# Pacing a transformer's FFN pieces by their TensorE time, and projecting the second head group while rows are still being normalised

## The chip, the cores and the metric

One core of one Trainium2 chip. The metric is the time of the whole program on the device, in microseconds (us), median of several runs.

## The reference

Two identical layers on one sequence of 2048 rows of 512 columns: attention with 32 heads of 16 columns, then a gated FFN of width 1792. The same weights serve both layers.

```python
def _A_ref(x, wqkv, wo):                       # attention, H = 32, Dh = 16
    q, k, v = split_heads(x @ wqkv)            # (shortened)
    p = softmax(q @ k.T * Dh ** -0.5)
    return (p @ v).merge_heads() @ wo

def _B_ref(x, w_gate, w_up, w_down):           # FFN, F = 1792
    return (gelu(x @ w_gate) * (x @ w_up)) @ w_down

x = x + _A_ref(layernorm(x)); x = x + _B_ref(layernorm(x))
x = x + _A_ref(layernorm(x)); x = x + _B_ref(layernorm(x))
```

## The kernel before

The program is written by a scheduler in Python. It keeps a rough clock of every engine while it emits instructions, and at each step it decides what TensorE does next. What it emits is a fixed order per engine, with semaphores between the engines.

A unit is four heads times one block of 512 query rows. It has 64 score tiles of 128 keys by 512 queries. There are 8 units in a block, 4 blocks in a layer, 4096 tiles in all. A score tile is one matmul, then an exponential, then an accumulating matmul with V. Most exponentials run on ScalarE, three and two tiles at a time. Some tiles go to VectorE, which makes the exponential by integer arithmetic; such a tile needs four accumulating matmuls instead of one.

Everything else has to fit between the score tiles, in "pieces" of TensorE work with their evacuations on VectorE. There are three sources of pieces, asked in this order: `heads` (the first layer norm), `prep` (the projections Q, K and V), and `post` (all that follows the attention of a block: output projection, layer norm, gate, up, down, and the next layer norm). A piece is emitted only if its bank and inputs are ready and if it does not overrun the next score tile by more than its source's tolerance.

```python
SW, MM = 0.107, 0.216                      # the scheduler's costs, us
DVE_LATE = 2.0                             # VectorE gets a score tile if less late than this

def prep_list(layer):                      # order and gates of Q, K, V pieces  (cut)
    def kv(c, b, after_all=False):
        def gate():
            return ("xnt", layer, b) in have and (not after_all or started_all()) and (
                not layer or units_done[layer - 1] >= (NQB - 1) * NG + 2 * c + 2)
        ...
    def q(up):
        def gate():
            return ("xnt", layer, up // NCK) in have and (layer or not up or started_all()) and filled_units[0] >= ...
        ...
    for up in range(1, NU // 2):
        if up < NCK and up not in cl:
            for b in range(NQB):
                kv(up, b, layer == 0)      # head groups 1..3 of layer 0: after all rows are normalised
        ...

def post_source():
    while True:
        if posts:
            pace["on"], pace["n"] = True, 0
            ...
            for p in posts.pop(0):
                if p is not None:
                    pace["n"] += 1         # one per piece, whatever its length
                yield p
            ...

PIECES = 4 + 8 + 4 * NFT                   # 68 pieces of a post; NFT = 14

def behind():                              # pieces due by now, minus pieces done
    if not pace["on"]:
        return 0.0
    f = (tiles_filled[0] / (4.0 * NKT) - NG * (posts_done[0] + 1) - 1.0) / (NG - 1.5)
    return PIECES * f - pace["n"]

def post_tol():
    if pace["haste"] or behind() > LAG:    # LAG = 24
        return 99.0
    return 1.0 if behind() > 0 else 0.1

sources = [Source(heads(), lambda: 0.1), Source(prep_source(), lambda: 0.1), Source(post_source(), post_tol)]

while True:                                # main loop  (cut)
    ...                                    # a score tile if one is ready, or accumulating matmuls
    cand = None
    for src in sources:
        p = src.peek()
        if p is None:
            continue
        bs = piece_banks(p)
        if bs is None or piece_ready(p, bs) > t + 0.02 or p.cost + change("full") > limit + src.tol():
            continue
        cand = (src, p, bs)
        break
    ...                                    # else more accumulating matmuls, or a zero-adding filler
```

Of the kernel before, what the change touches and what calls it, by code (L numbers as in the profile page):

```python
# [175 lines left out]
def _emit_fast(nc, es, x_in, wqkv, wo, wg, wu, wd, out, n_rep=2):  # L176
# [12 lines left out]
    NCK = D // 128  # L189
    NG = 2 * NCK  # L190
    NFT = F // 128
# [4 lines left out]
    NU = NQB * NG  # L196
# [40 lines left out]
    NQS = 6  # L237
# [43 lines left out]
    SW, MM = 0.107, 0.216  # L281
# [192 lines left out]
    pace = {"on": False, "n": 0, "haste": False}  # L474
    have = set()
# [152 lines left out]
    def qproj(layer, up):  # L628

        qb, c = up // NCK, up % NCK  # L630

        def evac(b):
            ops = []
            for p in range(2):
                slot = (layer * NU + 2 * up + p) % NQS
                ops.append((lambda e, p=p, slot=slot: e.tensor_scalar(Q[:, slot, :], bank(b), QMASK[:, p:p + 1], None,  # L636
                                                                     op0=ALU.mult),
                            [BK[b], ("QMASK",)], [("Q", slot)], 0.62))
            evac_job(1, b, ops, got((layer, "q", up)))
        return mm_piece([(WQ[:, ck, 128 * c:128 * (c + 1)], XNT[:, ck, 512 * qb:512 * (qb + 1)]) for ck in range(NCK)],  # L640
                        xk(qb) + [("WQ", c)], evac)

    def kproj(layer, c, kb):
        return mm_piece([(WK[:, ck, 128 * c:128 * (c + 1)], XNT[:, ck, 512 * kb:512 * (kb + 1)]) for ck in range(NCK)],
                        xk(kb) + [("WK", c)],
                        lambda b: evac_job(1, b, [(lambda e: e.tensor_copy(KT[:, c, 512 * kb:512 * (kb + 1)], bank(b)),
                                                   [BK[b]], [("KT", c, kb)], 0.6)], got((layer, "k", c, kb))))
# [3 lines left out]
    def vproj(layer, c, kb):  # L651
        def fn(e, bs):
            for t in range(4):
                for ck in range(NCK):
                    tt = 4 * kb + t
                    ins = e.matmul(bank(bs[0])[:, 128 * t:128 * (t + 1)], lhsT=XNT[:, ck, tt * 128:(tt + 1) * 128],  # L656
                                   rhs=WV[:, ck, 128 * c:128 * (c + 1)], start=(ck == 0), stop=(ck == NCK - 1))
            return ins

        def then(o):  # L660
            have.add((layer, "v", c, kb))
            for part, (m0, m1) in (("A", (0, NMA)), ("B", (NMA, NM))):
                if m1 == m0 or kb != (3 * m1 - 1) // 4:
                    continue
                for ph in range(1, NPH):
                    dst = VD[:, c, ph - 1, :, 4 * m0:4 * m1, :]
                    src = AP(VP, (2 * c * NKT * 4 + 12 * m0 + 2) * VW,
                             [[VP[:].ap[0][0], 128], [NKT * 4 * VW, 2], [3 * VW, 4 * (m1 - m0)], [1, VW]])
                    job("pool", 2, [(lambda e, dst=dst, src=src, ph=ph: e.tensor_scalar(  # L669
                        dst, src, 2.0 ** (-ph / NPH), None, op0=ALU.mult),  # L670
                        [("VP", c, k) for k in range(kb + 1)] + [("VPONE",)], [("VD", c, part)],
                        0.46 + 0.039 * 4 * (m1 - m0))],
                        got((layer, "vd", c, part)) if ph == NPH - 1 else None)

        def after(bs):
            b = bs[0]
            evac_job(1, b, [(lambda e: e.tensor_copy(  # L677
                VP[:, c, :, 16 * kb:16 * kb + 16, 0:16].rearrange("p r k d -> p k r d"),
                bank(b).rearrange("p (k r d) -> p k r d", r=2, d=16)),
                             [BK[b]], [("VP", c, kb)], 0.6)], then)  # L680

        return Piece(0.064 * 4 * NCK, xk(kb) + [("WV", c)], fn, after)


    units_done = [0] * n_rep
    filled_units = [0]

    def started_all():
        return ("xnt", 0, NQB - 1) in have

    def prep_list(layer):
        items = []

        def add(gate, fn):
            items.append((gate, fn))
# [5 lines that stand above are left out]
            add(gate, lambda: kproj(layer, c, b))  # L701
            if b == 0 and c in cl:
                q(c)
            add(gate, lambda: vproj(layer, c, b))

        def q(up):
            def gate():
                return ("xnt", layer, up // NCK) in have and (layer or not up or started_all()) and filled_units[0] >= layer * NU + 2 * up + 2 - NQS
            add(gate, lambda: qproj(layer, up))

        lead = [b for b in range(NQB) if not layer or b < NQB - 1 or NQB == 1]
        cl = range(min(NCK, NPART // 2)) if layer else [0]
        for c in cl:
            for b in lead:
                kv(c, b)
        for b in range(NQB):
            if b not in lead:
                for c in cl:
                    kv(c, b)
        for up in range(1, NU // 2):  # L720
            if up < NCK and up not in cl:
                for b in range(NQB):
                    kv(up, b, layer == 0)
            if up not in cl:
                q(up)
        return items
# [307 lines left out]
    slot_no = [0]  # L1034
    tiles_filled = [0]
    LAG = 24
    pt_no = [0]
    dg = {"n": 0, "items": [], "uk": None, "done": [0]}
    pp_no = [0]
# [12 lines left out]
    def slot_cap():  # L1052
        bs = slot_banks()
        return len([b for b in bs if b not in held3])

    def vector_tile():

        if pace["haste"]:
            return False
        if not dg["items"] and pend.get(("PI", dg["n"] % NPI)):  # L1060
            return False
        late = max(0.0, sch.free["dve"] - now[0]) + sum(op[3] for j in jobs["dve"] for op in j[2])
        late += 0.6 * len(shifts)
        return late < DVE_LATE

    def vector_bank():
        if not free_banks:
            return None
        return min(free_banks, key=lambda b: (sch.ready("pe", w=[BK[b]]), b))
# [8 lines left out]
    def pick(look=False):  # L1078

        cap = slot_cap()  # L1080
        want_d = not look and started_all() and behind() < LAG and vector_tile()
        bd = vector_bank() if want_d else None
# [308 lines left out]
    for layer in range(n_rep):  # L1391
        prep.extend(prep_list(layer))
# [14 lines left out]
# [4 lines that stand above are left out]
                pace["haste"] = posts_done[0] % NQB == NQB - 1 and NQB > 1  # L1411
                for p in posts.pop(0):
                    if p is not None:
                        pace["n"] += 1
                    yield p
                posts_done[0] += 1
                pace["haste"] = pace["on"] = False
            else:
                yield None

    posts_done = [0]

    PIECES = 4 + 8 + 4 * NFT

    def behind():

# [6 lines that stand above are left out]
        if pace["haste"] or behind() > LAG:  # L1433
# [4 lines that stand above are left out]
    total_posts = n_rep * NQB  # L1438
    DENSE = 0.7
    log = {"idle": 0.0, "warm": 0}  # L1440

    while True:
# [40 lines left out]
        for src in sources:  # L1483
            p = src.peek()
# [7 lines left out]
        if cand:  # L1492
            src, p, bs = cand
# [775 lines left out]
def _build(nc, x_in, wqkv, wo, wg, wu, wd, out, n_rep=2, force_general=False):  # L2269

    with contextlib.ExitStack() as es:
        fast, flag = _emit_fast(nc, es, x_in, wqkv, wo, wg, wu, wd, out, n_rep=n_rep)
# [94 lines left out]
```

## Time and profile before

| | before |
|---|---|
| median, range | 1685.4 us, 1682.9 to 1685.6 |
| span of the profiled run | 1682.9 us |
| ScalarE: first exponential starts, last ends | 17.67 us, 1610.1 us |
| ScalarE busy with exponentials | 1487.9 us, 1302 instructions, 3253 tiles |
| ScalarE waits for score matmuls | 42.5 us in 71 gaps, longest 5.34; one of them, 3.90 us, stands before the first exponential |
| tail after the last exponential | 72.8 us |

From the page of the kernel before, the span, the busy time of each engine, and three groups of instructions. A group's columns are: line, engine, operation, output and input, shapes, count, then busy us, mean ns of one, then the idle time just before them and what ended it.

```profile
span 1682.9 us, 37093 instructions
...
PE 1576.2 (94%) x15611; PEld 492.6 (29%) x15670; DVE 1378.6 (82%) x2334; ACT 1561.6 (93%) x1348; POOL 203.4 (12%) x217
...
L1204 ACT ACTIVATE fPT<-fPS 128x1536 bf16<-128x1536 f32 (+1 forms) x1302 | 1487.9, 1284 | 46.3 <-PE fPS L1191 42.5
L1241 DVE TENSOR_SCALAR fPI<-fPS 128x512 int16<-128x512 f32 x843 | 571.0, 684 | 93.4 <-PE fPS L1191 87.6
...
L1344 PE MATMUL fPS<-fONB,fZV 128*17 128x512 f16 x2452 | 189.6, 385 | 2.3 <-POOL fQMASK L362 1.5
...
```

The reader should see two things. TensorE and ScalarE are both busy for nine tenths of the span, but not with work of the same kind: 2452 of TensorE's matmuls (189.6 us of its busy time) are fillers that add zero, so TensorE has room. ScalarE between its first and last exponential has almost none: its groups show 1487.9 us of exponentials and 46.3 us of idle time before them. The ScalarE timeline shows these gaps and what each waited for. Its columns are start, length, instruction, count of merged instructions, and in brackets the idle time before the first of them and its releaser.

```profile
...
47.52 23.20 ACT L1204 ACTIVATE fPT<-fPS 128x1024 bf16<-128x1024 f32 x21 [1.28 <-PE fPS L1191]
76.06 68.55 ACT L1204 ACTIVATE fPT<-fPS 128x1536 bf16<-128x1536 f32 x60 [5.34 <-PE fPS L1191]
145.66 3.71 ACT L1204 ACTIVATE fPT<-fPS 128x1536 bf16<-128x1536 f32 x3 [1.05 <-PE fPS L1191]
...
298.04 9.14 ACT L1204 ACTIVATE fPT<-fPS 128x1536 bf16<-128x1536 f32 x8 [0.40 <-PE fPS L1191]
307.66 5.97 ACT L1204 ACTIVATE fPT<-fPS 128x1536 bf16<-128x1536 f32 x5 [0.47 <-PE fPS L1191]
313.65 1.28 ACT L1157 ACT_TABLE_LOAD   x1
314.94 6.27 ACT L1157 ACTIVATE fHT<-fHT 128x3584 bf16<-128x3584 bf16 x2
...
821.87 5.54 ACT L1204 ACTIVATE fPT<-fPS 128x1024 bf16<-128x1024 f32 x5 [4.79 <-PE fPS L1191]
...
```

The larger gaps are 1.28, 5.34, 1.05 and 0.91 us in the first 151 us, 4.79 us at 817 to 822 us, where the second layer begins, and two of 1.07 and 1.18 us later. The lines from 298 to 315 us show the other kind: gaps of 0.4 us one after another in the stretch before a GELU. (The last lines of that stretch also price the change of activation table: a load of 1.28 us between the exponential and the GELU.)

What TensorE does at the 5.34 us gap, from its timeline:

```profile
...
72.48 1.04 PE L592 MATMUL fPS<-fXNT,fWQ 128*128 128x512 f16 x4
73.35 1.03 PE L592 MATMUL fPS<-fXNT,fWK 128*128 128x512 f16 x4
74.21 1.06 PE L656 MATMUL fPS<-fWV,fXNT 128*128 128x128 bf16 x16
75.61 0.40 PE L1191 MATMUL fPS<-fQ,fKT 32*128 32x512 f16 x4 [0.34 <-DVE fKT L646]
...
```

Q, K and V of the second head group are projected one after the other, VectorE evacuates Q (two products from 73.55 us, 1.41 us together) and K (fKT, 0.68 us from 74.88), and only then does a score tile follow, at 75.61 us. The first two units hold 128 tiles and are used up here.

### The profile page before, as it was taken

The page shows a single profiled execution, that of the slowest core. Times are in us where ns is not written, and L with a number is a line of the kernel's source. Part 1 is how long each engine was busy: PE and PEld are TensorE (multiplying, and loading weights), DVE is VectorE, ACT ScalarE, POOL GpSimd, SP SyncE. Part 2 cuts the span into 40 slices and gives each one's busy share as a digit, 9 for nine tenths or more (in the row PEclk, how much of TensorE's full clock was granted, in tenths as well). Part 3 has the DMA queues.
Part 4 walks back from the last instruction along what each step waited for, and adds up shares of the span by engine and source line. Part 5 has one row for each costly group of instructions (what it writes and reads, how often), then busy time and mean ns, then how long its engine had stood idle before and what let it go on. Part 6 is the DMA issues. An engine that isn't in the chain of part 4 may idle for free.

```text
span 1682.9 us, 37093 instructions
## 1 busy us (share of the span) xinstructions
PE 1576.2 (94%) x15611; PEld 492.6 (29%) x15670; DVE 1378.6 (82%) x2334; ACT 1561.6 (93%) x1348; POOL 203.4 (12%) x217
## 2 busy tenths in 40 slices
PE   9999989999999989999999999999989999999998
PEld 3332222222222223233332322222222222222233
DVE  7899998888998899977643899988899878897852
ACT  6899999999999999999899999999999999999922
POOL 2312011101201021000600211101011100201000
PEclk9999999999999999999999999999999999999999
DMA  4100001252013410125214000024301251014303
GB/s 138 52 2 19 2 19 33 61 164 73 17 43 119 144 42 10 41 66 170 74 57 138 26 19 17 21 58 136 108 19 39 68 166 57 17 45 146 109 15 109
DMA packets 140286, 111.82 MB, mean 66 GB/s; under 512 B 13905, under 2 KB 129873, under 8 KB 140113
## 3 DMA queue, kind: packets, MB, share of 16 engines
q1 hardware_dynamic: 136416, 104.78, 21.3%
q0 software_dynamic: 2112, 4.19, 0.9%
q8 instruction: 127, 2.08, 0.5%
q10 hardware_dynamic: 1584, 0.39, 0.1%
q14 instruction: 47, 0.38, 0.1%
HBM read 97.78 MB, written 6.82 MB: 62 GB/s over the span
## 4 chain that ended last, share of the span: by engine, by line
ACT 52%; PE 35%; DVE 10%; DMA 1%; issue 1%; SPq 1%; POOL 0%; POOLq 0%; DVEq 0%
ACT fPT L1204 49%; PE fPS L592 11%; PE fPS L1324 9%; PE fPS L1191 9%; DVE fPP L1277 4%; PE fPS L953 4%; DVE fPI L1241 3%; ACT fHT L1157 2%; PE fPS L1344 2%; DVE fHT L939 1%; SPq L277 1%; DVE fHT L916 1%; ACT L1157 1%; PE fPS L656 1%; DVE fQ L636 0%
## 5 line engine op out<-in xcount | busy, mean ns | idle before, releaser
L1204 ACT ACTIVATE fPT<-fPS 128x1536 bf16<-128x1536 f32 (+1 forms) x1302 | 1487.9, 1284 | 46.3 <-PE fPS L1191 42.5
L1241 DVE TENSOR_SCALAR fPI<-fPS 128x512 int16<-128x512 f32 x843 | 571.0, 684 | 93.4 <-PE fPS L1191 87.6
L1191 PE MATMUL fPS<-fQ,fKT 32*128 32x512 f16 x4096 | 513.2, 384 | 50.0 <-ACT fPT L1204 36.3
L1324 PE MATMUL fPS<-fPT,fVP 128*17 128x512 bf16 x3253 | 469.0, 382 | 11.7 <-DVE fOS L829 5.6
L1277 DVE TENSOR_SCALAR fPP<-fPI 128x2048 int16<-128x2048 int16 (+3 forms) x723 | 444.7, 645 | 8.1 <-PE fPS L1324 2.3
L1324 PE MATMUL fPS<-fPP,fVD 128*17 128x512 f16 x2529 | 409.7, 381 | 10.8 <-DVE fPP L1277 5.9
L1191 PEld LDWEIGHTS fPS<-fQ,fKT 32*128 32x128 f16 x4096 | 129.0, 91 | 533.7 <-ACT fPT L1204 382.4
L1324 PE MATMUL fPS<-fPI,fVP 128*17 128x512 f16 x843 | 255.0, 382 | 2.0 <-DVE fPP L1277 1.5
L592 PE MATMUL fPS<-fXNT,fWR 128*128 128x512 f16 x896 | 221.7, 381 | 10.4 <-DVE fHT L939 6.0
L1344 PE MATMUL fPS<-fONB,fZV 128*17 128x512 f16 x2452 | 189.6, 385 | 2.3 <-POOL fQMASK L362 1.5
L1324 PEld LDWEIGHTS fPS<-fPT,fVP 128*17 128x17 f16 x3253 | 108.7, 88 | 163.4 <-issue 91.6
L788 POOL TENSOR_TENSOR fAT<-fOS,fRB 128x512 f16<-128x512 f32 x32 | 41.3, 1291 | 817.2 <-DMA fRB<-rscr 791.6
L1324 PEld LDWEIGHTS fPS<-fPP,fVD 128*17 128x17 f16 x2529 | 99.3, 88 | 120.7 <-issue 48.5
L939 DVE TENSOR_TENSOR fHT<-fPS,fHT 128x512 bf16<-128x512 f32 x112 | 76.4, 689 | 57.8 <-PE fPS L592 41.4
L953 PE MATMUL fPS<-fWR,fHT 128*128 128x512 bf16 x402 | 113.5, 382 | 7.2 <-issue 5.7
L592 PEld LDWEIGHTS fPS<-fXNT,fWR 128*128 128x128 bf16 x896 | 72.8, 98 | 128.3 <-DVE fHT L939 19.6
L916 DVE CAST fHT<-fPS 128x512 bf16<-128x512 f32 x98 | 66.6, 687 | 25.6 <-PE fPS L592 25.2
L1344 PEld LDWEIGHTS fPS<-fONB,fZV 128*17 128x17 f16 x2452 | 57.8, 91 | 66.5 <-issue 31.2
L1324 PEld LDWEIGHTS fPS<-fPI,fVP 128*17 128x17 f16 x843 | 58.3, 88 | 38.0 <-issue 13.9
L669 POOL TENSOR_SCALAR fVD<-fVP 128x544 f16<-128x544 f16 (+1 forms) x48 | 54.7, 1142 | 97.0 <-DVE fVP L677 94.4
L548 POOL TENSOR_SCALAR fLNS<-fMV 128x4 f32<-128x4 f32 (+1 forms) x17 | 5.2, 307 | 434.8 <-DVE fMV L541 434.7
L788 POOL TENSOR_TENSOR fATS<-fOS,fRB 128x512 f16<-128x512 f32 x32 | 42.3, 1323 | 78.2 <-DMA fRB<-rscr 78.2
(60 smaller groups left out, 697.9 us busy)
## 6 DMA issues: line engine op xcount, KB each, us to landing
fWR<-in_B_w_down_dram SPq DMA_DIRECT2D x189, 256.0 KB, 3.0
fWR<-in_B_w_gate_dram SPq DMA_DIRECT2D x56, 256.0 KB, 3.3
fWR<-in_B_w_up_dram SPq DMA_DIRECT2D x56, 256.0 KB, 2.9
fRB<-rscr SPq DMA_DIRECT2D x256, 32.0 KB, 1.8
fX<-in_A_x_dram POOLq DMA_DIRECT2D x4, 1024.0 KB, 5.6
xscr<-fX SPq DMA_DIRECT2D x16, 256.0 KB, 2.5
fX<-xscr SPq DMA_DIRECT2D x4, 1024.0 KB, 5.7
fAT<-fATS SPq DMA_DIRECT2D x128, 16.0 KB, 1.8
```

The lines of the kernel that those rows point to most:

```text
L592: ins = e.matmul(bank(bs[0])[:, 0:cols], lhsT=l, rhs=r_, start=(i == 0), stop=(i == n - 1))
L669: job("pool", 2, [(lambda e, dst=dst, src=src, ph=ph: e.tensor_scalar(dst, src, 2.0 ** (-ph / NPH), None, op0=ALU.mult), [("VP", c, k) for ...
L788: job("pool", 1, [(lambda e: e.tensor_tensor(dst, OS[:, os_, :], RB[:, slot, :], op=ALU.mult), [("OS", os_)] + [("RB", slot, j) for j in r ...
L916: evac_job(1, b, [(lambda e: e.tensor_copy(HT[:, ft, :], bank(b)), [BK[b]], [("HT", ft)], 0.6)], got(("gate", layer, qb, ft)))
L939: (lambda e: e.tensor_tensor(HT[:, ft, :], bank(b), HT[:, ft, :], op=ALU.mult), [BK[b], ("HT", ft)], [("HT", ft)], 0.62)], got(("up", laye ...
L953: ins = e.matmul(bank(b)[:, 0:D], lhsT=HT[:, ft, i * 128:(i + 1) * 128], rhs=WR[:, s, jj * D:(jj + 1) * D], start=(ft == 0), stop=(ft == N ...
L1191: ins = e.matmul(bank(b), lhsT=KT[32 * j:32 * j + 32, (u % NG) // 2, kt * 128:(kt + 1) * 128], rhs=Q[32 * j:32 * j + 32, (layer * NU + u) ...
L1204: o = sch.op("act", lambda e: e.activation(PT[:, p, 0:512 * na].rearrange("p (a b) -> p a b", a=na), PS[:, b0:b0 + na, :], ACTF.Exp, scale ...
L1241: dve(0, [(lambda e: e.tensor_scalar(PI[:, gi, 512 * r:512 * (r + 1)], bank(bd), DBIAS, 0.0, op0=ALU.add, op1=ALU.max), [BK[bd]], [("PI", ...
L1277: shifts.append((s, [(lambda e: e.tensor_scalar(PP[:, s, 0:512 * n], PI[:, gi, 0:512 * n], int(OCT) * ph // NPH, None, op0=ALU.add), [("PI ...
L1324: ins = e.matmul(PS[32 * j:32 * j + VW, ACC, :], lhsT=l, rhs=r_, start=a, stop=z, tile_position=(0, 32 * j), skip_group_check=True)
L1344: ins = e.matmul(PS[32 * j:32 * j + VW, ACC, :], lhsT=ZV[:, :], rhs=ones, start=False, stop=False, tile_position=(0, 32 * j), skip_group_c ...
```

## The change

Two things. First, K and V of the second head group for the first two blocks of rows, and its Q, may be projected before all rows are normalised. Second, a post's progress is counted in TensorE time instead of pieces: a gate or up piece (four matmuls of 512 columns) counts (0.864 + 0.1) / 0.71 = 1.36, a down piece 0.75, a transpose 0.48. The total stays the same, 68.3 against 68. The intent is that a post's TensorE load is spread evenly over the block.

```diff
+    PRE = 1
@@ prep_list
-                return ("xnt", layer, up // NCK) in have and (layer or not up or started_all()) and filled_units[0] >= layer * NU + 2 * up + 2 - NQS
+                return ("xnt", layer, up // NCK) in have and (layer or up < 2 or started_all()) and filled_units[0] >= layer * NU + 2 * up + 2 - NQS
@@
-                    kv(up, b, layer == 0)
+                    kv(up, b, layer == 0 and (up > 1 or b > PRE))
@@ post_source
-                        pace["n"] += 1
+                        pace["n"] += (p.cost + 0.1) / 0.71
@@
-    PIECES = 4 + 8 + 4 * NFT
+    PIECES = (4 * (4 * MM + 0.1) + 8 * (0.06 * NCK + 0.1) + 2 * NFT * (4 * MM + 0.1) + 2 * NFT * (2 * MM + 0.1)) / 0.71
```

More of the change, by code (lines that the diff above doesn't have):

```diff
@@ L1036, in _emit_fast @@
     LAG = 24
+    PRE = 1
     pt_no = [0]
```

## The prediction

> **What bounds it now.** From the first exponential (17.7 us) to the last (about 1610 us) ScalarE is the limit. The page's groups give 1302 exponentials, 1487.9 us of overlap-free busy time: 0.457 us per 512-column tile over 3253 tiles. In the table of waits ScalarE waited only 42.5 us for score matmuls, in 71 gaps. TensorE's 94% is not the bound: [...] 2452 of its matmuls are zero-adding filler. Before 17.7 us, and after 1610 us (72 us, the last block's FFN), the change touches little.
>
> **The 42.5 us of gaps** (ScalarE timeline): 5.34 us at 71-76 us; 1.28 at 47; two of about 1.0 at 145-150; 4.79 us at 817-822 (change of layer) and 1.07 after it; the rest, about 28 us, is some 65 gaps of 0.15-0.8 us, crowded into the gate phases before each GELU.
>
> **Change 1, the head.** The first two units hold 128 tiles. At tile 128 TensorE runs Q, K and V of the second head group in a row (72.5-75.1 us), VectorE evacuates, and ScalarE starves 5.34 us. In the changed kernel's order of instructions K, V, Q of block 0 stand at tiles 5-13 and K, V of block 1 at tiles 28-58, replacing filler (168 fewer). The head's last transposes stand at tile 58 instead of 60, so normalisation is not delayed. I expect 5 us, perhaps 1 more at 145 us.
>
> **Change 2, the pacing.** The total is the same (68 pieces, 68.3 equivalents now), but a gate or up piece counts 1.36, a down piece 0.75, a transpose 0.48: gate/up pieces get wider spacing, down pieces closer.
> - VectorE takes 832 tiles instead of 843, ScalarE 3264 instead of 3253. Estimate: 11 x 0.457 = 5 us more, straight on ScalarE's chain. Building each part alone shows that pacing causes ten of the eleven.
> - Fewer short gaps in the gate phases: perhaps 28 to 22 us, gain 6.
> - At the change of layer (tile 2080) more projections stand before the next score tile: K V K V K V, 16 transposes, K V K, against V K V, 8 transposes, K V. At about 0.97 us each, the 4.8 us gap could grow to 7-8: loss 3.
>
> **Sum.** -5.3 -1 (head) +5 (tiles) -6 (gaps) +3 (layer change) = -4. From 1685.6: **1681 us**, range **1672 to 1691**. Chances: faster by over 2% 0.01, within 2% 0.98, slower 0.01. About 75% that it is faster at all.
>
> **What would show each step.** Head: no ScalarE gap over 2 us at 60-80 us. Tiles: 1306 exponentials, busy about 1493 us. Gaps: waits for score matmuls fall from 42.5 to 33-35 us. Layer change: one gap of 6-8 us near 815 us. Tail after the last exponential: 72 us, within 1.
>
> **What would make it wrong.** If the gate gaps come from banks or from VectorE's evacuations rather than from crowding by pieces, pacing gains nothing and the change is worth -1 to 0. If the layer-change gap doesn't grow, or the gate gaps almost vanish, it is 8-12 us faster. If the second group's evacuations (four casts of 0.69 us, two Q products of 0.74 us) push back the head's statistics on VectorE, the gap at 47 us grows and eats the gain. [...]

Two passages are cut out of the recorded text, where it is marked: a general remark on matmul busy time, and a guess about VectorE's lateness on the chip, neither shown by a trace or run here. The sum: it came to -4.3 us, from 1685.6 to 1681 us. Its 0.97 us a projection agrees with the step from the start of a Q or K piece to the score tile behind it in the trace of the kernel before (K: 809.70 to 810.67 us); projections directly behind each other stepped by 0.86 to 0.90 us (816.21 to 817.07 and 817.07 to 817.97).

## More of the kernel before

What TensorE does at the change of layer, and when GpSimd has the normalised rows (fHT) that the transposes (L569, into the normalised transposed input) need:

```profile
...
814.39 0.62 PE L569 MATMUL fPS<-fIDN,fHT 128*128 128x128 f16 x8
814.94 0.39 PE L1191 MATMUL fPS<-fQ,fKT 32*128 32x512 f16 x3
...
817.97 0.61 PE L569 MATMUL fPS<-fIDN,fHT 128*128 128x128 f16 x8
...
819.58 1.04 PE L592 MATMUL fPS<-fXNT,fWK 128*128 128x512 f16 x4 [0.46 <-DVE fXNT L583]
...
821.44 0.60 PE L1191 MATMUL fPS<-fQ,fKT 32*128 32x512 f16 x5
...
```

```profile
...
812.49 3.04 POOL L562 TENSOR_SCALAR fHT<-fX,fLNS 128x512 f16<-128x512 f32 x4
...
```

The last of the second layer's first 32 score tiles, those that need only the keys of the first two blocks of rows, starts at 814.94 us. The next ones need K of the third block of rows, which needs those rows normalised and transposed. The rows are ready at 815.5 us; the second half of the transposes runs at 817.97, the K at 819.58, the score tiles at 821.44.

## The result, and the profile after

| | before | after |
|---|---|---|
| median, range | 1685.4 us, 1682.9 to 1685.6 | 1684.8 us, 1683.4 to 1689.1 |
| ratio, 95% interval | | 1.0001 (0.9984 to 1.0019) |
| the same, repeated with five rounds | | 1.0016 (1.0003 to 1.0029) |
| span of the profiled run | 1682.9 us | 1681.6 us |

The change moved the time by nothing that one set of runs can tell, and by +0.16% in the second. It is not faster.

From the page of the changed kernel, the same lines as above (two lines were added to the source, so L1204 is L1206 now, and so on):

```profile
span 1681.6 us, 36670 instructions
...
PE 1573.4 (94%) x15414; PEld 492.3 (29%) x15469; DVE 1374.2 (82%) x2320; ACT 1564.7 (93%) x1352; POOL 202.4 (12%) x217
...
L1206 ACT ACTIVATE fPT<-fPS 128x1536 bf16<-128x1536 f32 (+1 forms) x1306 | 1491.1, 1291 | 43.9 <-PE fPS L1193 41.4
L1243 DVE TENSOR_SCALAR fPI<-fPS 128x512 int16<-128x512 f32 x832 | 563.8, 684 | 110.6 <-PE fPS L1193 107.0
...
L1346 PE MATMUL fPS<-fONB,fZV 128*17 128x512 f16 x2284 | 173.1, 384 | 2.5 <-POOL fQMASK L362 1.5
...
```

There are 168 fillers fewer, 11 score tiles fewer on VectorE, and four exponentials more. The granted clock was no lower without these 168 fillers: the page of the profile shows 90% or more in all 40 slices of both kernels, and the mean was 0.999 before and 1.000 after.

The ScalarE timeline after:

```profile
...
48.27 98.44 ACT L1206 ACTIVATE fPT<-fPS 128x1024 bf16<-128x1024 f32 x87 [1.28 <-PE fPS L1193]
...
291.19 9.14 ACT L1206 ACTIVATE fPT<-fPS 128x1536 bf16<-128x1536 f32 x8 [0.39 <-PE fPS L1193]
300.81 5.97 ACT L1206 ACTIVATE fPT<-fPS 128x1536 bf16<-128x1536 f32 x5 [0.47 <-PE fPS L1193]
...
819.12 5.54 ACT L1206 ACTIVATE fPT<-fPS 128x1024 bf16<-128x1024 f32 x5 [9.25 <-PE fPS L1193]
...
```

The gap at 76 us is gone: the exponentials from 48.27 to 146.7 us are one line, with no gap between them that the timeline shows. The gaps of 0.4 us before the first GELU (291 and 301 us) stand there as before, within a hundredth. The gap at the change of layer is 9.25 us, where it was 4.79. TensorE there, and GpSimd:

```profile
...
808.10 0.39 PE L1193 MATMUL fPS<-fQ,fKT 32*128 32x512 f16 x2
808.41 1.04 PE L592 MATMUL fPS<-fXNT,fWK 128*128 128x512 f16 x4
809.29 1.06 PE L656 MATMUL fPS<-fWV,fXNT 128*128 128x128 bf16 x16
810.18 1.03 PE L592 MATMUL fPS<-fXNT,fWK 128*128 128x512 f16 x4
811.04 1.06 PE L656 MATMUL fPS<-fWV,fXNT 128*128 128x128 bf16 x16
811.94 1.03 PE L592 MATMUL fPS<-fXNT,fWK 128*128 128x512 f16 x4
812.80 1.06 PE L656 MATMUL fPS<-fWV,fXNT 128*128 128x128 bf16 x16
813.70 1.06 PE L569 MATMUL fPS<-fIDN,fHT 128*128 128x128 f16 x16
...
815.97 1.04 PE L592 MATMUL fPS<-fXNT,fWK 128*128 128x512 f16 x4 [0.68 <-DVE fXNT L583]
...
818.69 0.39 PE L1193 MATMUL fPS<-fQ,fKT 32*128 32x512 f16 x2
...
```

```profile
...
800.74 4.71 POOL L562 TENSOR_SCALAR fHT<-fX,fLNS 128x512 f16<-128x512 f32 x4
...
```

Now the rows are ready at 805.45 us, ten microseconds earlier than before, and for eight microseconds nothing uses them: after the last score tile at 808.10 six projections stand in TensorE's order (K, V, K, V, K, V, 5.3 us from 808.41 to 813.70), then the 16 transposes, then the K that the score tiles wait for. The transposes ran in their place in the order: the first started at 813.70 us, 8.25 us after their rows were ready.

The change of the span, term by term. The waits are sums of the bracketed gaps of the ScalarE timeline, which add up to the totals of the table of waits (42.5 and 41.4 us; both have 3.90 us before the first exponential in them, which cancel):

| term | before | after | change |
|---|---|---|---|
| start of the first exponential | 17.67 | 16.97 | -0.7 |
| exponentials' busy time | 1487.9 | 1491.1 | +3.2 |
| waits for score matmuls up to the first GELU | 15.7 | 10.0 | -5.7 |
| the same, third to fourth GELU (change of layer) | 8.0 | 10.4 | +2.4 |
| the same, everywhere else | 18.7 | 20.9 | +2.2 |
| other idle time before exponentials (46.3 - 42.5; 43.9 - 41.4) | 3.8 | 2.5 | -1.3 |
| tail after the last exponential | 72.8 | 71.4 | -1.4 |
| sum | | | -1.3 |

The sum is the difference of the two spans, -1.3 us; the start and the tail, -2.1 us together, belong to no line of the change and vary like this from run to run (first exponential at 16.5 to 18.1 us, tail 71.0 to 73.4 us over the profiles).

### The profile page after: what moved, and what is told of

Read it like the earlier page. It is cut to its first block, busy times and chain, and to the rows that moved or that the text cites. A ratio compares the mean times of both kernels' runs of the same rounds, so it can differ in the third digit from the quotient of the medians.

```text
span 1681.6 us, 36670 instructions
## 1 busy us (share of the span) xinstructions
PE 1573.4 (94%) x15414; PEld 492.3 (29%) x15469; DVE 1374.2 (82%) x2320; ACT 1564.7 (93%) x1352; POOL 202.4 (12%) x217
## 4 chain that ended last, share of the span: by engine, by line
ACT 60%; PE 29%; DVE 10%; issue 1%; POOL 0%; DVEq 0%; POOLq 0%
ACT fPT L1206 57%; PE fPS L592 9%; PE fPS L1193 7%; PE fPS L1326 7%; DVE fPP L1279 4%; DVE fPI L1243 4%; PE fPS L1346 3%; PE fPS L954 2%; ACT fHT L1159 2%; DVE fHT L940 1%; PE fPS L656 1%; DVE fHT L917 1%; ACT L1159 1%; PE fPS L569 0%; POOL fVD L669 0%
## 5 line engine op out<-in xcount | busy, mean ns | idle before, releaser
L1206 ACT ACTIVATE fPT<-fPS 128x1536 bf16<-128x1536 f32 (+1 forms) x1306 | 1491.1, 1291 | 43.9 <-PE fPS L1193 41.4
L1243 DVE TENSOR_SCALAR fPI<-fPS 128x512 int16<-128x512 f32 x832 | 563.8, 684 | 110.6 <-PE fPS L1193 107.0
L1193 PE MATMUL fPS<-fQ,fKT 32*128 32x512 f16 x4096 | 518.9, 384 | 56.4 <-ACT fPT L1206 35.8
L1326 PE MATMUL fPS<-fPT,fVP 128*17 128x512 bf16 x3264 | 475.8, 383 | 16.2 <-DVE fOS L830 7.8
L1326 PE MATMUL fPS<-fPP,fVD 128*17 128x512 f16 x2496 | 419.9, 381 | 9.1 <-DVE fPP L1279 5.8
L1346 PE MATMUL fPS<-fONB,fZV 128*17 128x512 f16 x2284 | 173.1, 384 | 2.5 <-POOL fQMASK L362 1.5
L1346 PEld LDWEIGHTS fPS<-fONB,fZV 128*17 128x17 f16 x2284 | 54.4, 91 | 61.9 <-issue 24.8
L830 DVE COPY fOS<-fPS 128x512 f32<-128x512 f32 x64 | 43.9, 685 | 10.6 <-PE fPS L1326 9.8
```

The lines of the kernel that those rows point to most:

```text
L1193: ins = e.matmul(bank(b), lhsT=KT[32 * j:32 * j + 32, (u % NG) // 2, kt * 128:(kt + 1) * 128], rhs=Q[32 * j:32 * j + 32, (layer * NU + u) ...
L1206: o = sch.op("act", lambda e: e.activation(PT[:, p, 0:512 * na].rearrange("p (a b) -> p a b", a=na), PS[:, b0:b0 + na, :], ACTF.Exp, scale ...
L1243: dve(0, [(lambda e: e.tensor_scalar(PI[:, gi, 512 * r:512 * (r + 1)], bank(bd), DBIAS, 0.0, op0=ALU.add, op1=ALU.max), [BK[bd]], [("PI", ...
L1326: ins = e.matmul(PS[32 * j:32 * j + VW, ACC, :], lhsT=l, rhs=r_, start=a, stop=z, tile_position=(0, 32 * j), skip_group_check=True)
L1346: ins = e.matmul(PS[32 * j:32 * j + VW, ACC, :], lhsT=ZV[:, :], rhs=ones, start=False, stop=False, tile_position=(0, 32 * j), skip_group_c ...
```

## The experiments

Theory A: the head's gap is really removed, worth about 5 us; the pacing gives it back, by more tiles on ScalarE and by the order of the pieces at the change of layer. Rival B: the early projections only move work, and the gain is lost again whatever the pacing. Rival C: at the change of layer it is not the order of the pieces that makes the gap but late rows or VectorE's evacuations. Rival D (from the runs with another `DVE_LATE` on): a tile taken off ScalarE comes back as waits.

All kernels gave correct results. Counts of tiles and places of pieces ("at tile 2080") come from the order of instructions of the built kernels. The runs were made in three batches of four on different chips, each beside the kernel before, so across batches the ratios are compared and not the times. Of the first batch (the two parts alone and the two rules on transposes) a second profile of each kernel exists. The gap at the change of layer is the same in both to 0.01 us; smaller gaps are not always.

### One part alone: the head

The first three changed lines of the diff above, without the pacing.

> Only the head part of the change; pacing as before. Theory A (the head's gap is really removed, and the changed kernel loses the gain again through the pacing): about 1680 us, 5 to 6 us under the kernel before; no ScalarE gap over 2 us at 60 to 80 us; the gap at the change of layer stays 4.5 to 5.5 us; exponentials 1302, busy 1488 within 1. Rival B (work only moved: the projections done early push later work back, and the gain at 76 us is given back inside the first block whatever the pacing): the gap at 76 us goes, but new gaps of about 5 us in sum appear before the first GELU, and the time stays 1684 to 1686.

Measured: 1682.5 us (1679.3 to 1683.1), ratio 0.9987 (0.9974 to 1.0001). The gap at 76 us is gone and the waits up to the first GELU are 9.4 us instead of 15.7, as expected. The gap at the change of layer is 4.79 us, to the hundredth as before; exponentials 1302, busy 1488.1. But the time fell by about 2 us, not by 5 to 6 (the interval just reaches 1, so even that is at the edge of the noise), and the sum of waits by 2.8 us only (39.7). Two stretches gave some back: 1.3 us between the second and the third GELU, and 2.3 us around the change of layer, where two new gaps of 1.28 and 1.34 us stand at 832 and 835 us. TensorE's timeline there:

```profile
...
830.51 1.23 PE L592 MATMUL fPS<-fWO,fAT 128*128 128x512 bf16 x4 [1.28 <-DMA fAT<-fATS]
...
```

TensorE waited 1.28 us for a transfer of attention rows (in the kernel before it waited 0.65 us at the same piece), and score tiles stood behind it in the order. A second profile of this kernel (span 1677.6 us) does not have these two gaps, and TensorE waited 0.23 us at that piece. Its waits up to the first GELU are 9.4 us again and its sum is 39.4, but there 1.7 us come back between the second and the third GELU and 1.9 between the fourth and the fifth. So neither theory was quite right: the gain is real up to the first GELU, and about half of it is lost later, not in the first block as B said, and without the pacing's help. Where it is lost differs from run to run; why is not shown.

### One part alone: the pacing

The last two changed lines of the diff, without the head part.

> Only the pacing part; head as before. Theory A: slower than before by 4 to 8 us (1689 to 1693): ten more tiles on ScalarE (3 to 5 us) and a gap of about 9 us instead of 4.8 at the change of layer (4 us), with the short gaps before the GELUs about as large as before (24 us). Rival B (the pacing is neutral and the head gives nothing): within 1 us of the kernel before.

Measured: 1690.0 us (1688.6 to 1691.7), ratio 1.0036 (1.0022 to 1.0050), same rounds as the run before. Slower by 6 us, as A said. Exponentials 1306, busy 1491.0 us (+3.1); gap at the change of layer 9.25 us against 4.79 (+4.5). Rival B's "within 1 us" falls. The pacing is the part that costs, and the head part hides it.

Why did the pacing not spread the load? The starts of the pieces can be read from the traces, and ScalarE's waits between them summed. For the first post, gate and up pieces (first and last start of that line from 200 to 480 us, the last one in the next post) and down pieces, before and then after:

```profile
...
L592 PE MATMUL fPS<-fXNT,fWR x140: 378/379/391, 266.1 to 479.0; 128*128 128x512 f16 x140
...
L953 PE MATMUL fPS<-fWR,fHT x50: 378/379/391, 347.0 to 388.2; 128*128 128x512 bf16 x50
...
```

```profile
...
L592 PE MATMUL fPS<-fXNT,fWR x148: 379/379/390, 259.2 to 479.3; 128*128 128x512 f16 x148
...
L954 PE MATMUL fPS<-fWR,fHT x50: 379/379/391, 340.9 to 382.9; 128*128 128x512 bf16 x50
...
```

So from the first gate piece to the first down piece it is 80.9 us before and 81.7 after. The last post of each layer is not paced (its tolerance is 99). Over the other six:

| six paced posts | before | after |
|---|---|---|
| first gate piece to first down piece, post by post, us | 80.9, 74.7, 80.4, 73.7, 75.1, 68.0 | 81.7, 81.3, 83.9, 73.0, 82.5, 73.8 |
| start of the first to start of the last gate piece, sum of six | 243.3 us | 237.5 us |
| the same for the up pieces | 162.9 us | 183.6 us |
| ScalarE's waits, first gate piece to first up piece | 10.3 us in 28 gaps | 14.0 us in 39 |
| ScalarE's waits, first up piece to first down piece | 5.5 us in 12 gaps | 2.4 us in 6 |

The new weight meant 36% wider. The gate pieces did not get wider at all, the up pieces by 13%. The pacing alone shows the same (waits of 13.6 and 1.5 us). Counters printed by the scheduler while building show why: `behind()` was above zero at every gate piece in both kernels (in the first post 6.4 at the first gate piece before and 6.7 after). While it is between 0 and 24 the tolerance is 1.0, whatever its value, and it never reached 24. So the gate pieces went out as fast as they fitted between score tiles in both kernels. Before, this held for the up pieces too; in the changed kernel the counter fell to or below zero at 40 of the 84 up pieces (at the first down piece of the first post it was 8.6 before and 0.7 after), and there the spacing widened and the waits fell. Most of the short gaps, though, stand at the gate pieces, where the weights changed only which small decisions came out differently. What makes the gaps there is open, but it is not simply how close the gate pieces stand: in the run with `DVE_LATE = 2.4` on the kernel before (below) they stand closer (219.5 us) and ScalarE waits less there (6.1 us).

Built with other constants in place of 0.1 (0.0 to 3.0), the pacing alone gave VectorE between 797 and 841 tiles, against 843 before: 841 at 0.2, 833 at 0.1 and at 0.3, 797 at 3.0. Every constant lost some tiles, with no clear rule among the small ones. Why the weights lose tiles is not shown; this rests on counts, not on runs.

### Transposes first when ScalarE starves

On the changed kernel:

```diff
-        for src in sources:
+        order = sources
+        if F is None and sources[2].peek() is not None and sources[2].peek().cost == 0.06 * NCK:
+            order = [sources[2]] + sources[:2]
+        for src in order:
             p = src.peek()
```

`F is None` means that no score tile can be filled; the cost is that of a transpose.

> The changed kernel with one rule more: when no score tile can be filled, a post's transposes go before projections. In the order of instructions this puts the 16 transposes ahead of the six K and V pieces at tile 2080 and sends the next score tiles after one K and one V. Theory A (the normalised rows lay ready for 8 us behind those six pieces of 0.9 us each): gap at the change of layer falls from 9.25 to 2.5 to 4 us; two tiles more on ScalarE cost 1; time 1678 to 1681, about 5 us under the changed kernel. Rival C (the rows or VectorE's evacuations are what ends the gap): the gap stays over 7 us and the time within 1 us of the changed kernel.

Measured: 1681.4 us (1678.4 to 1684.3), at the upper edge of what A expected; ratio to the kernel before 0.9987 (0.9974 to 1.0001). ScalarE's and TensorE's timelines:

```profile
...
812.77 9.15 ACT L1206 ACTIVATE fPT<-fPS 128x1024 bf16<-128x1024 f32 x8 [3.17 <-PE fPS L1193]
...
```

```profile
...
807.83 0.39 PE L1193 MATMUL fPS<-fQ,fKT 32*128 32x512 f16 x2
808.15 1.22 PE L569 MATMUL fPS<-fIDN,fHT 128*128 128x128 f16 x16
...
809.62 1.90 PE L592 MATMUL fPS<-fXNT,fWK 128*128 128x512 f16 x8
811.36 1.06 PE L656 MATMUL fPS<-fWV,fXNT 128*128 128x128 bf16 x16
...
```

The gap is 3.17 us instead of 9.25, and the transposes start right behind the last score tile. The rows were ready at 805.2 us, as in the changed kernel, so rival C falls for this kernel: the order made the larger part of the gap. All waits together fell from 41.4 to 36.4 us, a little less than the gap did. Later stretches came out differently: the waits before the sixth GELU fell from 4.7 to 1.9 us, those before the seventh grew from 2.6 to 6.5 us (in the second profile, with 34.1 us in all, to 3.8).

Repeated beside the changed kernel itself, in the same rounds:

> The changed kernel itself once more, in the same rounds as the next three, to compare them directly. Both theories: 1683 to 1687, ratio to the kernel before 0.999 to 1.001; gap at the change of layer 9 to 9.5 us, exponentials 1306.

> The changed kernel with transposes before projections when no score tile can be filled, once more, now beside the changed kernel itself. Theory A (order of the pieces makes the larger half of the gap): 3 to 5 us under the changed kernel of these rounds, gap 3 to 3.5 us. Rival: within 1 us of it.

Measured: the changed kernel 1686.2 us, ratio 1.0016 (1.0003 to 1.0029), a little over what was expected, gap 9.25 us; with the rule 1681.6 us, ratio 0.9985 (0.9973 to 0.9998), gap 3.17 us. The rule is worth 0.31% (1.0016 - 0.9985), about 5 us, the upper end of the range expected.

### Transposes first all through the third post

```diff
+        if posts_done[0] == NQB - 2 and sources[2].peek() is not None and sources[2].peek().cost == 0.06 * NCK:
```

in place of the condition on `F`.

> The changed kernel, with transposes ahead of projections throughout the third block's post of the first layer (nowhere else). In the order of instructions the transposes then stand at tiles 2062 to 2068 and the K that tile 2080 needs at tile 2074. Theory A: no gap over 1.5 us at the change of layer; six tiles more on ScalarE cost up to 2.7 us; time about 1677 to 1680. Rival C: a gap of over 5 us remains near 815 us since rows or evacuations end it, time 1684 to 1687.

Measured: 1683.0 us (1680.8 to 1685.7), ratio 0.9997 (0.9983 to 1.0010). A miss for A as stated: a gap of 3.49 us remains at 812 us, and one of 2.47 us comes at 843 us. The transposes did run early (805.4 to 808.2 us), so what remains is something else. TensorE's timeline:

```profile
...
810.34 0.39 PE L1326 MATMUL fPS<-fPT,fVP 128*17 128x512 bf16 x2 [1.29 <-DVE fOS L830]
...
811.53 0.61 PE L1193 MATMUL fPS<-fQ,fKT 32*128 32x512 f16 x6
...
```

TensorE stood 1.29 us before an accumulating matmul, for VectorE's copy of the finished accumulator (fOS), and the score tiles were behind that. The copy itself waited for VectorE, which ran three shifts for its own tiles from 807.71 to 809.6 us. With one wait taken away, the next in TensorE's order showed. The second profile has the same wait of 1.29 us. The gap at 843 us follows a wait of TensorE for a transfer of attention rows (2.90 us). The time missed A's 1677 to 1680 as well as C's 1684 to 1687.

### Projections with the post's tolerance

The changed kernel with

```diff
-    sources = [..., Source(prep_source(), lambda: 0.1), ...]
+    sources = [..., Source(prep_source(), lambda: 1.0 if posts_done[0] == NQB - 2 else 0.1), ...]
```

> The changed kernel; while the third block's post of the first layer runs, projections may overrun the next score tile by 1.0 us, as that post's pieces already may. In the order of instructions K, V, K, V of the next layer then go back to tiles 1933 to 1951 (they slipped to 2064 to 2080 in the changed kernel) and six instead of nine pieces stand between tile 2080 and the next. Exponentials and tiles are the same as in the changed kernel (1306, 3264), so only the gap can move the time. Theory A (crowded-out projections make the gap): gap 5 to 7 us instead of 9.25, time 2 to 4 us under the changed kernel, about 1681 to 1682. Rival C (the post's late rows make it): gap over 8.5, time within 1 us of the changed kernel's 1684.8.

Measured: 1692.0 us (1685.7 to 1694.4), ratio 1.0033 (1.0013 to 1.0053): slower than the changed kernel, and the gap is 8.31 us. Theory A's expectation failed. GpSimd and VectorE show why:

```profile
...
813.72 3.02 POOL L562 TENSOR_SCALAR fHT<-fX,fLNS 128x512 f16<-128x512 f32 x4
...
```

```profile
...
807.11 0.68 DVE L983 TENSOR_TENSOR fX<-fPS,fX 128x512 f32<-128x512 f32 x1
...
```

With the projections done earlier, the post came later: its last addition (L983) is at 807.11 us (796.76 in the changed kernel) and the rows are ready at 816.7 us, where the changed kernel had them at 805.45. Here the rows are late, as rival C has it, though C's numbers (gap over 8.5 us, time within 1 us) missed too. My reading, not tested further: TensorE has a fixed amount of work to do before tile 2080; whichever of the two goes first, the other is late. What helped, in the first rule on transposes, was to give the pieces that the next score tile needs their place; giving one source more room did not help. The time is not explained by the gap, which is shorter than the changed kernel's. All waits are 44.9 us against 41.4. Two more things of this run stay open: its exponentials' busy time is 2.5 us over the changed kernel's for the same tiles (1493.6 against 1491.1), and its six times fall into two groups, two near 1686 and four from 1691.6 to 1694.4 us (the profile is of one of the four).

### The price of a tile, and candidates

On the kernel before:

```diff
-    DVE_LATE = 2.0
+    DVE_LATE = 2.4
```

> The kernel before, with VectorE allowed to be 2.4 us late instead of 2.0 when it is offered a score tile. In the order of instructions this moves 23 tiles from ScalarE to VectorE (3230 against 3253; 1292 exponentials); nothing else is meant to change. It prices a tile: Theory A (a tile on ScalarE costs its 0.457 us of chain): exponentials' busy time 1477 to 1479, time about 10 us less, 1674 to 1676, if the gaps stay at 42 us. Rival D (TensorE, which has three more accumulate matmuls for each such tile, or VectorE takes it back as waits): gaps before exponentials grow by 5 us or more and the time stays above 1681.

Measured: 1681.3 us (1680.6 to 1682.8), ratio 0.9982 (0.9969 to 0.9995). Busy time of the exponentials 1480.3 us, 7.6 less for 23 tiles: 0.33 us a tile, where I had expected 0.457. The waits grew from 42.5 to 46.6 us (7.14 us at 76 us, 6.81 at the change of layer). So D is right in part: some of it comes back.

The head part, the rule on transposes, and `DVE_LATE = 2.4` together:

> A candidate: the head part alone, transposes before projections when no score tile can be filled, and VectorE allowed 2.4 us late; 3231 tiles on ScalarE. If the three effects add (head -2 to -5, tiles -10, gap at the change of layer 3 to 4 instead of 4.8): 1669 to 1673. If VectorE's lateness comes back as gaps (rival D): 1678 to 1684.

Measured: 1676.4 us (1675.1 to 1678.0), ratio 0.9951 (0.9938 to 0.9965). Between the two expectations: busy 1481.7 us, waits 39.7, gap 3.09 at the change of layer.

The same without the rule on transposes:

> The best candidate so far without its rule on transposes (head part, VectorE allowed 2.4 us late; 3231 tiles). In the order of instructions eight pieces stand at tile 2080 against four with the rule. Theory A: gap at the change of layer 6 to 8 us, time 1679 to 1681, 3 to 4 us over the candidate with the rule. Rival C (rows end the gap): as with the rule, 1676 within 1.

Measured: 1681.2 us (1676.4 to 1683.4), ratio 0.9976 (0.9964 to 0.9989), gap at the change of layer 6.81 us. By the ratios the rule is worth about 4 us here too. A's gap held; the time and the difference are at or just over the upper edge of its numbers.

The head part with `DVE_LATE = 2.6`, no rule:

> A candidate: the head part alone with VectorE allowed 2.6 us late; 3221 tiles on ScalarE, 32 fewer than before. Theory A: tiles -14.6, head -2 to -5: 1666 to 1670 with gaps unchanged. Rival D: gaps over 55 us in sum and 1678 or more.

Measured: 1694.9 us (1693.3 to 1696.1), ratio 1.0062 (1.0049 to 1.0075). Busy time fell by 9.4 us, to 1478.5, and not by the 14.6 expected. The waits sum to 58.6 us, and the gap at the change of layer alone is 18.25 us: the transposes ran only from 821.4 us, because the rows came late (the post's last down matmuls on TensorE start at 815.32 us, and from 815.86 it ran 100 fillers, 5.58 us, up to the first transposes). D's numbers held. Fewer tiles on ScalarE gained nothing in this run, since the schedule they came with delayed the rows.

The whole change with `DVE_LATE = 2.4` and the rule:

> The whole change with VectorE allowed 2.4 us late and transposes first: 3242 tiles on ScalarE; in the order of instructions nothing but score tiles, one K or V at a time and fillers stands around tile 2080 (transposes at 2031 to 2057, the K it needs by 2071). Theory A (tiles and the change of layer are the whole price of the pacing): no gap over 2 us at the change of layer, busy time about 1486, time 1674 to 1678. Rival (pacing costs in its own right): 1680 or more.

Measured: 1666.9 us (1664.5 to 1669.3), ratio 0.9901 (0.9887 to 0.9916), the fastest kernel, and 7 us under what A expected. Its line of the page and its ScalarE timeline at the change of layer:

```profile
...
L1206 ACT ACTIVATE fPT<-fPS 128x1536 bf16<-128x1536 f32 (+1 forms) x1297 | 1482.9, 1280 | 32.5 <-PE fPS L1193 28.6
...
```

```profile
...
752.18 53.28 ACT L1206 ACTIVATE fPT<-fPS 128x1024 bf16<-128x1024 f32 x47 [0.16 <-PE fPS L1193]
805.78 48.71 ACT L1206 ACTIVATE fPT<-fPS 128x1536 bf16<-128x1536 f32 x42 [0.32 <-PE fPS L1193]
...
```

There is no gap over 0.4 us from 740 to 880 us, and the waits are 28.6 us against 42.5. It has more tiles on ScalarE than the best candidate with the head part alone (3242 against 3231) and is still 8 to 9 us faster (0.9901 against 0.9951): in the profiles its waits are 11.1 us fewer. So the pacing need not cost anything: what it cost in the change goes with the schedule that came out at the change of layer, and with the tiles. Whether the pacing gives this kernel anything, or whether it only happens to have a good schedule, these runs do not settle.

## Why the prediction was right or wrong

The predicted time, 1681 us with a range of 1672 to 1691, held: measured 1684.8 and, repeated, 1686.2 us. "Within 2%" held. Both were wide enough to hold with a step wrong. The sign did not: I gave 75% for faster at all, and the change is level or slightly slower.

| term of the sum | predicted | measured |
|---|---|---|
| head, waits up to the first GELU | -6.3 | -5.7 |
| tiles on ScalarE | +5 | +3.2 |
| short gaps in the gate phases | -6 | +2.2 (all waits outside the first block and the change of layer); +0.6 in the gate and up phases of the six paced posts |
| change of layer | +3 | +2.4 in that stretch; the gap itself +4.5 |

- **Head: right.** No gap over 2 us at 60 to 80 us, no delay of the rows. What I did not foresee is that alone it is worth only about 2 us, because later waits take part of it back: in one profile behind a transfer, in another elsewhere. What decides this is not shown.
- **Tiles: right in direction, mis-sized.** Exponentials 1306 as told, busy 1491.1 instead of 1493 us. The mean of 0.457 us a tile was too much for the marginal tile: 3.2 us for 11 tiles is 0.29 us, and the run with `DVE_LATE = 2.4` on the kernel before gives 0.33. Between runs of equal tiles busy time differed by up to 2.9 us (1490.7 to 1493.6), so this price is rough.
- **Change of layer: right in mechanism, the gap larger than told** (9.25 us against 6 to 8). I counted the pieces in the order of instructions and was right that they would stand in the way; the rule on transposes showed that their order, and not late rows, makes 6 us of it in this kernel.
- **The step that failed: "gate/up pieces get wider spacing", and with it "fewer short gaps in the gate phases".** I took the diff's intent for its effect. The counter is read only against 0 and 24. It was above zero at every gate piece in both kernels, so these were spaced as before (243.3 and 237.5 us in sum), and ScalarE's waits among them grew from 10.3 to 14.0 us. Only among the up pieces, 13% wider, did they fall, from 5.5 to 2.4. All waits came to 41.4 us where I had told 33 to 35. The term was also mis-sized: these phases held 15.9 us of waits and not about 28, which had the 3.90 us before the first exponential in it. Why the waits at the gate pieces grew stays open.

In the table this term missed by 8.2 us and the sum by only 3 (-1.3 in the profiles against -4.3). The rest was made up mostly by the tiles and, for 3.4 us, by the start, the tail and other idle time, which no step was about. That the time came so near was luck in part.

## What to carry to other kernels

Before costing a change to a pacing rule, check in the trace whether the rule was limiting anything: here the spacing of the gate pieces was already set by what fits, and the new weights hardly moved it (243.3 and 237.5 us in sum). A gap that closed showed other waits behind it (with the head part alone 5.34 us closed and the waits fell by 2.8 us in sum; with transposes first in the third post the gap of 9.25 us became one of 3.49, and one of 2.47 us came at 843 us), so price a gap by an experiment that removes it alone. Where the limiting engine starves at a boundary, list the pieces that its next instruction needs and put those first; here that was worth about 5 us, more than the head part alone.
